# Rounding of 64-bit weights in three stages, with ScalarE's results in the score buffers, inside a fused attention and feed-forward kernel

## The chip, the cores and the metric

The kernel runs on one core of a Trainium2 chip. The metric is the device time of one execution in microseconds (us); the median of three runs is compared. A profile of one further execution shows what each engine did: PE (TensorE), DVE (VectorE), ACT (ScalarE), POOL (GpSimd) and the queue SP that issues the DMAs.

## The reference

The reference is a routed attention followed by a feed-forward block, all in fp32. There are 4 batches, 8 heads, 768 positions and a head dimension of 64.

```python
q_assign = argmax(q_n @ c_n)                    # 16 centroids per head; k_assign likewise
mask     = q_assign[:, :, :, None] == k_assign[:, :, None, :]
attn     = softmax(where(mask, q @ k.T / 8, -1e9))
x        = (attn @ v) laid out as (3072 tokens, 512)
h        = x @ w_in                             # 512 x 2048
out      = (h * sigmoid(1.702 * h)) @ w_out     # 2048 x 512
```

The two weight matrices reach the kernel as 64-bit floats. The kernel has to turn each into 32-bit floats before PE can use it, and it does that with integer operations on the two 32-bit halves.

## The kernel before

**Units and turns.** A *unit* is 128 keys against half of the queries (384) for a pair of heads. `scores(u)` is two matrix products into a PSUM tile `s` of 128x2x512 (two banks; the pool `ps_s` has two such tiles). For the first batch `part(u)` adds the mask with two small products of one-hot rows; `exps(u)` is ScalarE's exponential, which writes the SBUF tile `A`. For the later batches `exps` writes back into `s`, and `mask(u)` on VectorE makes `A` from it. GpSimd adds the six `A` of a group to `sum` (L430). `values(u)` multiplies `A` with the values; after the sixth unit ScalarE copies the result to `x` (L446). A *turn* `t` is two units; there are 96 turns, 24 for each batch, and three turns make a group.

**Order within a turn.** The program is an order written out by hand, turn by turn: every engine runs its instructions in the order in which this loop issues them. In a turn come the two `scores`, the two `part`, the two `exps`, then `mask`, the `values` of the turn before, and a list of preparations for later pairs of heads (`prep_turn`: transposes of queries and keys, L262 and L267; `prep_near` and `prep_assign`: the nearest centroid, L276 to L308; `prep_hot`: one-hot rows, L349 to L356). Once in three turns, at t = 4, 7, 10 and so on, `normalise(g)` sums over the keys with a product by ones (L453), takes VectorE's reciprocal `rec` (L456) and scales `x` (L458). `check(g)` then lets ScalarE form two sums over `rec` (L468, L470) that tell at the end whether the fast path holds. Last come the feed-forward chunks.

**Feed-forward.** Each half batch makes 28 chunks: 16 times `first` (four products with `w_in`, L487, then tanh, L492, and a product on VectorE, L494), and 12 times `second` (four products with `w_out`, L504). The chunks of a half batch enter the queue `ffn` at its last `normalise`, the first at t = 13; `rate` chunks (2.43) are taken per turn. Products, transposes and the rest share three PSUM banks `m` (`ps_m`).

**Rounding.** The weights are 32 pieces of 128x512, the first 16 of `w_in`. `load_w(i)` brings in a piece with its two halves interleaved (`raw`). `split_w` takes out the exponent `e` and the mantissa bits on VectorE (L159, L161) and converts both on ScalarE (L163, L165). `join_w` puts sign, exponent, and both parts of the mantissa together on VectorE (L171, L174, L177). All of it lies in SBUF. One `round_next()` is `split_w(i)` and then `join_w(i - 1)`. It is called once in most turns from t = 1 to 10, and from t = 12 two or three times a turn:

```python
        second = t >= TB // 2          # TB = 24
        if second:
            round_next()               # after the exps of the turn
...
        if second or t and t % 4 != 3:
            round_next()               # after preparations and normalise
...
        if second and t % 2:
            round_next()               # after the feed-forward chunks
```

`first` and `second` call `round_to(n)`, which rounds at once what a chunk needs and is not yet rounded.

Of the kernel before, what the change touches and what calls it, by code (L numbers as in the profile page):

```python
# [8 lines left out]
FP32 = mybir.dt.float32  # L9
BF16 = mybir.dt.bfloat16  # L10
I32 = mybir.dt.int32
U32 = mybir.dt.uint32
U8 = mybir.dt.uint8
AF = mybir.ActivationFunctionType
ALU = mybir.AluOpType
# [23 lines left out]
def fast(  # L39
# [21 lines left out]
    nc = tc.nc  # L61
# [4 lines left out]
    P = 128  # L66
    NJ = S // P
    HALF = S // 2
    NH = NJ // 2
# [3 lines left out]
    NF = DF // P  # L73
# [10 lines left out]
    wp = ctx.enter_context(tc.tile_pool(name="wp", bufs=3))  # L84
# [7 lines left out]
        name="dram", bufs=2, space=bass.MemoryType.DRAM))  # L92
    ps_s = ctx.enter_context(tc.tile_pool(name="ps_s", bufs=2, space=PS))
# [4 lines left out]
    def bank():  # L98
        return ps_m.tile([P, 512], FP32, name="m")

    def short():
        return tmp.tile([P, HALF], FP32, name="short")
# [14 lines left out]
    def load_v(p):  # L117
# [15 lines left out]
    WN = 512  # L133
    w_chunks = [
        (w[:, c, n:n + WN],
         src.bitcast(I32)[c * P:(c + 1) * P, 2 * n:2 * (n + WN)])
        for w, src, n_c, n_n in ((w_in, moe_w_in, NCH, DF),
                                 (w_out, moe_w_out, NF, DM))
        for n in range(0, n_n, WN) for c in range(n_c)]
    NW = len(w_chunks)  # L140
    w_raw, w_pow = {}, {}

    def load_w(i):
        if i < NW:
            t = wp.tile([P, WN, 2], I32, name="raw")
            nc.sync.dma_start(out=t.rearrange("p n t -> p (n t)"),
                              in_=w_chunks[i][1])
            w_raw[i] = t
# [2 lines left out]

    EXP = 0x7FF00000

    def split_w(i):

        hi = w_raw[i][:, :, 1]
        w = w_chunks[i][0]
        e = wp.tile([P, WN], I32, name="e")
        nc.vector.tensor_scalar(out=e, in0=hi, scalar1=EXP, scalar2=None,  # L159
                                op0=ALU.bitwise_and)  # L160
        nc.vector.tensor_scalar(out=w.bitcast(I32), in0=hi, scalar1=0xFFFFF,  # L161
                                scalar2=None, op0=ALU.bitwise_and)
        nc.scalar.activation(out=e, in_=e, func=AF.Relu, scale=8.0,  # L163
                             bias=low[:, 0:1])
        nc.scalar.activation(out=w, in_=w.bitcast(I32), func=AF.Copy,  # L165
                             scale=2.0 ** -20, bias=1.0)
        w_pow[i] = e

    def join_w(i):
        raw, e, w = w_raw.pop(i), w_pow.pop(i), w_chunks[i][0]  # L170
        nc.vector.scalar_tensor_tensor(  # L171
            out=e, in0=raw[:, :, 1], scalar=-2 ** 31, in1=e,
            op0=ALU.bitwise_and, op1=ALU.bitwise_or)
        nc.vector.scalar_tensor_tensor(  # L174
            out=w, in0=raw.bitcast(U32)[:, :, 0], scalar=2.0 ** -52, in1=w,
            op0=ALU.mult, op1=ALU.add)
        nc.vector.tensor_tensor(out=w, in0=w, in1=e.bitcast(FP32),  # L177
                                op=ALU.mult)

    w_done = [0]  # L180

    def round_next():
        i = w_done[0]
        if i < NW:
            load_w(i + 2)
            split_w(i)
        if 0 < i <= NW:
            join_w(i - 1)
        w_done[0] += 1

    def round_to(n):
        while w_done[0] <= min(n, NW):
            round_next()

    load_qk(1, 0)
    load_v(0)
# [8 lines left out]
    low = const.tile([P, 1], FP32, name="low")  # L205
# [25 lines left out]
                            op0=ALU.add)  # L231
# [3 lines left out]
    for a in range(2):  # L235
        nc.vector.tensor_scalar(out=cc[:, a, :], in0=cent,
                                scalar1=crec[:, 0:1], scalar2=None,
                                op0=ALU.mult)
# [5 lines left out]
    for a in range(2):  # L244
        rows = slice(a * D, (a + 1) * D)
        nc.vector.tensor_copy(
            out=cT[rows, :, a, :],
            in_=cps[rows, 0:P].rearrange("d (h a c) -> d h a c", a=2,
                                         c=NC)[:, :, a, :])
# [128 lines left out]
    def scores(u):  # L378
        g, kt = divmod(u, NJ)
        p, h = split(g)  # L380
        ps = ps_s.tile([P, 2, 512], FP32, name="s")
        for a in range(2):
            rows = slice(a * D, (a + 1) * D)
            nc.tensor.matmul(out=ps[:, a, 0:HALF],  # L384
                             lhsT=T[p, 1][rows, kt * P:(kt + 1) * P],
                             rhs=T[p, 0][rows, h * HALF:(h + 1) * HALF],
                             start=True, stop=(p >= HP))
        s_of[u] = ps[:, :, 0:HALF]

    def part(u):  # L390

        g, kt = divmod(u, NJ)
        p, h = split(g)
        if p >= HP:
            return
        for a in range(2):
            r = 32 * (2 * (p % 2) + a)
            nc.tensor.matmul(  # L398
                out=s_of[u][:, a, :],
                lhsT=hots[p // 2, 1][r:r + NC, kt * P:(kt + 1) * P],  # L400
                rhs=hots[p // 2, 0][r:r + NC, h * HALF:(h + 1) * HALF],
                start=False, stop=True)

    def exps(u):
        p, h = split(u // NJ)
        s = s_of[u]
        if p < HP:
            A_of[u] = ap.tile([P, 2, HALF], FP32, name="A")
        nc.scalar.activation(out=A_of[u] if p < HP else s, in_=s, func=AF.Exp,  # L409
                             scale=SCALE)  # L410
# [37 lines left out]
    def normalise(g):  # L448

        sm = sum_of.pop(g)  # L450
        ps = bank()
        for a in range(2):
            nc.tensor.matmul(out=ps[a * D:(a + 1) * D, 0:HALF], lhsT=ones,  # L453
                             rhs=sm[:, a, :], start=True, stop=True)
        rec = recs[g] = short()
        nc.vector.reciprocal(out=rec, in_=ps[:, 0:HALF])  # L456
        x = xT_of[g] = O_of.pop(g)
        nc.vector.tensor_tensor(out=x, in0=x, in1=rec, op=ALU.mult)  # L458
        if g % HP == HP - 1:
            ffn.extend(ffn_chunks(g // HP))  # L460

    recs = {}

    def check(g):


        rec = recs.pop(g)
        nc.scalar.activation(out=rec, in_=rec, func=AF.Copy,  # L468
                             accum_out=sums[:, 0, g:g + 1])
        nc.scalar.activation(out=rec, in_=rec, func=AF.Relu, bias=top[:, 0:1],  # L470
                             scale=-2.0 * LIMIT * LIMIT,
                             accum_out=sums[:, 1, g:g + 1])


    ffn = deque()
# [47 lines left out]
    TG = NJ // 2  # L523
    TB = 2 * HP * TG

    prep_at = {}
    for p in range(1, NPAIR):
        b, hp = divmod(p, HP)
        for i in range(2 if p == 1 else 0, len(PREP)):
            if p == 1:  # L530
                t = (i - 2) // 2
            elif b == 0:
                t = (hp - 2) * TG + 1 + i // 2
            else:
                t = b * TB + (-20, -8, -2, 1)[hp] + i
# [5 lines left out]
    def prep(p, i):  # L541
        if i == 0 and p:
            load_v(p)
        PREP[i](p)
        if i in (1, 3) and loads:
            load_qk(*loads.popleft())

    rate = (NF + NH * (NF // 4)) / (TB / 2 - 0.5)
    owed = 0.0
    for p, i in [(0, i) for i in range(6)] + [(1, i) for i in range(2)]:  # L550
        prep(p, i)
# [2 lines left out]
    for t in range(NT + 2):  # L554
        us = range(2 * t, 2 * t + 2) if t < NT else ()
        for u in us:
            scores(u)
        if t == 0:
            prep(0, 6)
        for u in us:  # L560
            part(u)
        for u in us:
            exps(u)
        second = t >= TB // 2
        if second:
            round_next()
        for u in us:
            mask(u)
        work = sorted(prep_at.get(t, ()), key=lambda w: PREP[w[1]] != prep_near)
        while work and PREP[work[0][1]] == prep_near:  # L570
            prep(*work.pop(0))
        if 1 <= t <= NT:
            for u in range(2 * t - 2, 2 * t):
                values(u)
        owed = owed + rate if ffn else 0.0
        g = (t - 2) // TG if t >= 2 and (t - 2) % TG == TG - 1 else None
        if g is not None and second:
            normalise(g)
        for p, i in work:
            prep(p, i)  # L580
        if g is not None and not second:
            normalise(g)
        if recs:
            check(*recs)
        if second or t and t % 4 != 3:
            round_next()
        while owed >= 1 and ffn:
            ffn.popleft()()
            owed -= 1
        if second and t % 2:  # L590
            round_next()


    ok = const.tile([P, 2, 2 * NPAIR], FP32, name="ok")
    nc.vector.tensor_scalar(out=ok, in0=sums, scalar1=LIMIT, scalar2=None,
                            op0=ALU.is_le)
    ok1 = const.tile([P, 1], FP32, name="ok1")
    nc.vector.tensor_reduce(out=ok1, in_=ok, axis=AX.XY, op=ALU.min)
    for _ in range(NF // 2):
# [7 lines left out]
                            op0=ALU.mult, op1=ALU.add)  # L607
# [445 lines left out]
```

## Time and profile before

| | |
|---|---|
| median of the runs | 1089.02 us (1088.73 to 1090.47) |
| the profiled execution's own time | 1089.2 us |
| its span, first to last instruction | 1087.3 us |
| PE busy | 1049.0 us (96%) |
| DVE busy | 490.8 us (45%) |
| ACT busy | 354.8 us (33%) |
| POOL busy | 296.9 us (27%) |
| granted TensorE clock, mean | 0.99 |

The time of the profiled execution is its span and 1.9 us around it. A busy share is taken over the whole span, while rounding ends at about 193 us; so the first 220 us, the 24 turns of the first batch, are read apart from the rest. A matrix product's row shows how long it was under way, which overlaps with the next; how fast PE can go is read from the distance between starts.

### The profile page before, as it was taken

Reading aid. Unit: us, or ns where it says so; the run is one execution under the profiler, and the core shown is the slowest. Engines: PE = TensorE matmul, PEld = TensorE weight load, DVE = VectorE, ACT = ScalarE, POOL = GpSimd, SP = SyncE. Lnnn points to the kernel's source line nnn. Section 1 sums busy time; section 2 is a strip of 40 time slices with the busy share of each in tenths; the row PEclk is TensorE's granted clock in tenths of the full one; section 3 lists DMA queues with packets and bytes.
Section 4 is the critical chain, followed back from the end, with each engine's and each line's share of the span. In section 5 each row is a group of like instructions: output and inputs, shape, how many; then the busy total and the mean of one; then the engine's idle time right before and its main releaser. Section 6 shows DMA issues by size and latency. Waiting matters only on the chain. (4 is left out here: it accounts for less than half of the span.)

```text
span 1087.3 us, 10456 instructions
## 1 busy us (share of the span) xinstructions
PE 1049.0 (96%) x3982; PEld 492.6 (45%) x3982; DVE 490.8 (45%) x744; ACT 354.8 (33%) x665; POOL 296.9 (27%) x168
## 2 busy tenths in 40 slices
PE   7878799999999999999999999999999999999997
PEld 3423344445544455444454445444554445444543
DVE  3889999225442344424453164423552344431200
ACT  3755555223422333223432233223332133311100
POOL 2644223213232333123231142222332333230000
PEclk9998899999999999999999999999999999999999
DMA  7623443110100010002100000010000000000000
GB/s 199 165 81 116 131 133 111 46 49 17 49 23 27 10 30 15 31 25 54 51 23 17 15 20 15 15 48 32 8 7 12 10 10 1 1 10 20 1 11 22
DMA packets 64813, 45.13 MB, mean 42 GB/s; under 512 B 51953, under 2 KB 57585, under 8 KB 64753
## 3 DMA queue, kind: packets, MB, share of 16 engines
q1 hardware_dynamic: 64608, 44.33, 14.3%
q8 instruction: 33, 0.54, 0.2%
q14 instruction: 28, 0.22, 0.1%
q10 hardware_dynamic: 144, 0.03, 0.0%
HBM read 38.04 MB, written 6.31 MB: 41 GB/s over the span
## 5 line engine op out<-in xcount | busy, mean ns | idle before, releaser
L430 POOL TENSOR_TENSOR sum<-sum,A 128x768 f32<-128x768 f32 x128 | 235.5, 1840 | 461.3 <-DVE A L420 364.1
L487 PE MATMUL m<-x,w_in 128*128 128x384 f32 x1024 | 347.1, 494 | 9.7 <-ACT T L267 4.4
L504 PE MATMUL m<-w_out,g 128*128 128x512 f32 x768 | 337.8, 594 | 0.7 <-ACT short L282 0.7
L420 DVE SCALAR_TENSOR_TENSOR A<-qb,code,s 128x384 f32<-128x384 uint8 x288 | 157.6, 609 | 274.6 <-ACT s L409 251.9
L487 PEld LDWEIGHTS m<-x,w_in 128*128 128x128 f32 x1024 | 192.2, 192 | 149.1 <-issue 16.3
L504 PEld LDWEIGHTS m<-w_out,g 128*128 128x128 f32 x768 | 143.3, 190 | 175.6 <-issue 171.5
L494 DVE SCALAR_TENSOR_TENSOR g<-g,m 128x384 f32<-128x384 f32 x128 | 70.0, 553 | 220.4 <-ACT g L492 220.3
L384 PE MATMUL s<-T,T 64*128 64x384 f32 x768 | 152.9, 517 | 9.7 <-ACT A L409 9.6
L409 ACT ACTIVATE s<-s 128x768 f32<-128x768 f32 x144 | 107.9, 792 | 136.0 <-PE s L384 136.0
L441 PE MATMUL o<-A,inv 128*64 128x384 f32 x768 | 146.3, 502 | 0.0
L492 ACT ACTIVATE g<-m 128x384 f32<-128x384 f32 x128 | 61.7, 487 | 196.4 <-PE m L487 196.3
L430 POOL TENSOR_TENSOR sum<-A 128x768 f32<-128x768 f32 x32 | 60.0, 1876 | 215.6 <-DVE A L420 179.5
L384 PEld LDWEIGHTS s<-T,T 64*128 64x128 f32 x768 | 66.6, 189 | 94.6 <-issue 52.2
L456 DVE RECIPROCAL short<-m 128x384 f32<-128x384 f32 x32 | 81.6, 2551 | 25.8 <-PE m L453 25.8
L441 PEld LDWEIGHTS o<-A,inv 128*64 128x64 f32 x768 | 46.8, 137 | 84.8 <-issue 84.1
L510 ACT ACTIVATE y<-m 128x512 f32<-128x512 f32 x24 | 14.3, 595 | 155.8 <-PE m L504 142.7
L468 ACT ACTIVATE short<-short 128x384 f32<-128x384 f32 x32 | 16.7, 523 | 111.2 <-DVE x L458 111.2
L409 ACT ACTIVATE A<-s 128x768 f32<-128x768 f32 x48 | 36.1, 804 | 22.0 <-PE s L398 22.0
L267 ACT COPY T<-m 128x384 f32<-128x384 f32 x64 | 29.7, 480 | 37.2 <-PE m L262 37.1
L262 PE MATMUL m<-ident,in 128*128 128x128 f32 x192 | 33.9, 298 | 3.1 <-ACT T L267 1.7
L163 ACT ACTIVATE e<-e,low 128x512 int32<-128x512 int32 x32 | 23.1, 722 | 28.8 <-DVE e L159 28.8
L262 PEld LDWEIGHTS m<-ident,in 128*128 128x128 f32 x192 | 21.5, 146 | 22.4 <-issue 11.9
(68 smaller groups left out, 373.5 us busy)
## 6 DMA issues: line engine op xcount, KB each, us to landing
raw<-in_moe_w_in_dram SPq DMA_DIRECT2D x16, 512.0 KB
raw<-in_moe_w_out_dram SPq DMA_DIRECT2D x16, 512.0 KB
in<-in_q_dram SPq DMA_DIRECT2D x32, 192.0 KB
in<-in_k_dram SPq DMA_DIRECT2D x32, 192.0 KB
inv<-in_v_dram SPq DMA_DIRECT2D x16, 384.0 KB
out_dram<-y SPq DMA_DIRECT2D x24, 256.0 KB
qb<-line SPq DMA_DIRECT2D x12, 192.0 KB
line<-row SPq DMA_DIRECT2D x12, 1.5 KB
```

The source lines that it names most:

```text
L262: nc.tensor.transpose(out=ps[:, n * P:(n + 1) * P], in_=qk_in[p, w][:, h * NH + n].rearrange("p a d -> p (a d)"), identity=ident)
L267: nc.scalar.copy(dst, ps[:, 0:HALF])
L384: nc.tensor.matmul(out=ps[:, a, 0:HALF], lhsT=T[p, 1][rows, kt * P:(kt + 1) * P], rhs=T[p, 0][rows, h * HALF:(h + 1) * HALF], start=True, ...
L409: nc.scalar.activation(out=A_of[u] if p < HP else s, in_=s, func=AF.Exp, scale=SCALE)
L420: nc.vector.scalar_tensor_tensor(out=A_of[u][:, a, :], in0=qcode[p][:, a, h * HALF:(h + 1) * HALF], scalar=code[p][:, kt % NH, 1, kt // NH ...
L430: nc.gpsimd.tensor_tensor(out=sum_of[g], in0=A_of[u - 1] if kt == 1 else sum_of[g], in1=A, op=ALU.add)
L441: nc.tensor.matmul(out=o_of[g][a * D:(a + 1) * D, 0:HALF], lhsT=v_in[p][:, a, kt, :], rhs=A[:, a, :], start=(kt == 0), stop=(kt == NJ - 1))
L456: nc.vector.reciprocal(out=rec, in_=ps[:, 0:HALF])
L487: nc.tensor.matmul(out=ps[:, 0:HALF], lhsT=w_in[:, c, f * P:(f + 1) * P], rhs=xT[c], start=(c == 0), stop=(c == NCH - 1))
L492: nc.scalar.activation(out=g, in_=ps[:, 0:HALF], func=AF.Tanh, scale=0.851)
L494: nc.vector.scalar_tensor_tensor(out=g, in0=g, scalar=1.0, in1=ps[:, 0:HALF], op0=ALU.add, op1=ALU.mult)
L504: nc.tensor.matmul(out=ps[:, 0:DM], lhsT=hs[f][:, n * P:(n + 1) * P], rhs=w_out[:, f, :], start=(f == 0), stop=(f == NF - 1))
```

## The change

`split_w` and `join_w` become three steps. `take_w` loads ahead and takes `e` and the mantissa bits out on VectorE. `part_w` is ScalarE's two conversions; their results go to a tile `r` that is taken from the score pool `ps_s` (name `s`), after the turn's exponentials, instead of being written in place in SBUF. `join_w` reads `r` from PSUM, writes an intermediate back to it, and ends in the weights. From t = 12 two pieces are rounded per turn (before: two or three), and before that one piece is joined in a turn that has one. Each step of a piece stands apart in the turn. `check` moves from the end of the turn that normalises to behind the exponentials of the next turn. For t below 24 two chunks are taken per turn (`SLOW`), from then on 2.43 (`RATE`).

```diff
-    def split_w(i):
-
+    w_at = [0, 0, 0]
+
+    def take_w():
+        i = w_at[0]
+        if i >= NW or i > w_at[2] + 1:
+            return
+        load_w(i + 2)
         hi = w_raw[i][:, :, 1]
-        w = w_chunks[i][0]
-        e = wp.tile([P, WN], I32, name="e")
+        e = w_e[i] = wp.tile([P, WN], I32, name="e")
         nc.vector.tensor_scalar(out=e, in0=hi, scalar1=EXP, scalar2=None,
                                 op0=ALU.bitwise_and)
-        nc.vector.tensor_scalar(out=w.bitcast(I32), in0=hi, scalar1=0xFFFFF,
-                                scalar2=None, op0=ALU.bitwise_and)
-        nc.scalar.activation(out=e, in_=e, func=AF.Relu, scale=8.0,
-                             bias=low[:, 0:1])
-        nc.scalar.activation(out=w, in_=w.bitcast(I32), func=AF.Copy,
-                             scale=2.0 ** -20, bias=1.0)
-        w_pow[i] = e
+        nc.vector.tensor_scalar(out=w_chunks[i][0].bitcast(I32), in0=hi,
+                                scalar1=0xFFFFF, scalar2=None,
+                                op0=ALU.bitwise_and)
+        w_at[0] += 1
+
+    def part_w():
+        i = w_at[1]
+        if i >= w_at[0]:
+            return
+        r = w_r[i] = ps_s.tile([P, 2, WN], FP32, name="s")
+        nc.scalar.activation(out=r.bitcast(I32)[:, 0, :], in_=w_e[i],
+                             func=AF.Relu, scale=8.0, bias=low[:, 0:1])
+        nc.scalar.activation(out=r[:, 1, :], in_=w_chunks[i][0].bitcast(I32),
+                             func=AF.Copy, scale=2.0 ** -20, bias=1.0)
+        w_at[1] += 1
 
-    def join_w(i):
-        raw, e, w = w_raw.pop(i), w_pow.pop(i), w_chunks[i][0]
+    def join_w():
+        i = w_at[2]
+        if i >= w_at[1]:
+            return
+        raw, e, r, w = w_raw.pop(i), w_e.pop(i), w_r.pop(i), w_chunks[i][0]
         nc.vector.scalar_tensor_tensor(
-            out=e, in0=raw[:, :, 1], scalar=-2 ** 31, in1=e,
+            out=e, in0=raw[:, :, 1], scalar=-2 ** 31,
+            in1=r.bitcast(I32)[:, 0, :],
             op0=ALU.bitwise_and, op1=ALU.bitwise_or)
         nc.vector.scalar_tensor_tensor(
-            out=w, in0=raw.bitcast(U32)[:, :, 0], scalar=2.0 ** -52, in1=w,
-            op0=ALU.mult, op1=ALU.add)
-        nc.vector.tensor_tensor(out=w, in0=w, in1=e.bitcast(FP32),
+            out=r[:, 1, :], in0=raw.bitcast(U32)[:, :, 0], scalar=2.0 ** -52,
+            in1=r[:, 1, :], op0=ALU.mult, op1=ALU.add)
+        nc.vector.tensor_tensor(out=w, in0=r[:, 1, :], in1=e.bitcast(FP32),
                                 op=ALU.mult)
+        w_at[2] += 1
...
+    RATE = (NF + NH * (NF // 4)) / (TB / 2 - 0.5)
+    SLOW = 2.0
...
-        second = t >= TB // 2
-        if second:
-            round_next()
+        part_w()
+        if recs:
+            check(*recs)
         for u in us:
             mask(u)
...
-        owed = owed + rate if ffn else 0.0
+        second = t >= TB // 2
+        owed = owed + (RATE if t >= TB else SLOW) if ffn else 0.0
...
         if g is not None and second:
             normalise(g)
+        if second:
+            join_w()
+            take_w()
         for p, i in work:
             prep(p, i)
         if g is not None and not second:
             normalise(g)
-        if recs:
-            check(*recs)
-        if second or t and t % 4 != 3:
-            round_next()
+        if second:
+            part_w()
+        join_w()
+        if not second and t and t % 4 != 3:
+            take_w()
         while owed >= 1 and ffn:
             ffn.popleft()()
             owed -= 1
-        if second and t % 2:
-            round_next()
+        if second:
+            take_w()
...
+    check(*recs)
```

## The prediction, made before the run

> **What bounds the kernel now.** I read the page's slices first, then the table of stretches cut at turn starts, then the waits of the first batch, its timeline, and the groups by form.
>
> ```profile
> PE   7878799999999999999999999999999999999997
> ...
> DVE  3889999225442344424453164423552344431200
> ...
> PEclk9998899999999999999999999999999999999999
> ```
>
> PE is full but for the first seven slices and the end. DVE is full in slices 3 to 6.
>
> ```profile
> core 0: us, PE busy (x) PEld busy (x) DVE busy (x) ACT busy (x) POOL busy (x), PEclk, DMA share, GB/s
> 41.10:82.10 41.00, 30.95 (x200) 12.52 (x198) 35.27 (x50) 24.74 (x49) 19.77 (x11) 0.99 0.45 120
> 92.40:138.40 46.00, 35.20 (x125) 16.49 (x123) 44.22 (x59) 21.74 (x42) 13.52 (x7) 0.89 0.43 128
> 138.40:219.30 80.90, 79.89 (x313) 36.70 (x312) 55.50 (x82) 35.74 (x66) 22.62 (x12) 1.00 0.32 93
> 219.30:968.90 749.60, 746.89 (x2787) 351.65 (x2786) 311.95 (x478) 230.06 (x434) 213.44 (x118) 1.00 0.08 23
> ```
>
> From 219.3 us (turn 24) PE is busy for 746.9 of 749.6 us: whatever this change does to ACT, DVE or POOL there is worth under 3 us. The case is decided in turns 3 to 23. At turns 14 to 16 (92.4 to 138.4) DVE is busy for 44 of 46 us, PE for 35.
>
> ```profile
> ACT short L468 <- DVE x L458: 20.2, 5, 6.0
> ...
> PE s L384 <- ACT A L409: 9.6, 5, 4.0
> ```
>
> These waits of 40 to 140 us show ACT standing in `check` for the reciprocal, and PE's scores then waiting for late exponentials.
>
> ```profile
> 82.02 0.69 DVE L171 SCALAR_TENSOR_TENSOR e<-raw,e 128x512 int32<-128x512 int32 x1
> 82.19 4.39 POOL L430 TENSOR_TENSOR sum<-sum,A 128x768 f32<-128x768 f32 x2 [3.78 <-ACT A L409]
> 82.62 2.29 DVE L174 SCALAR_TENSOR_TENSOR w_in<-raw,w_in 128x512 f32<-128x512 uint32 x1
> 84.95 2.18 DVE L177 TENSOR_TENSOR w_in<-w_in,e 128x512 f32<-128x512 f32 x1
> ```
>
> The same DVE step takes 0.69 us or 2.3: the long ones end with a POOL sum.
>
> ```profile
> L171 DVE SCALAR_TENSOR_TENSOR e<-raw,e 128x512 int32<-128x512 int32 x32 | 25.2, 787 | 0.0
> L163 ACT ACTIVATE e<-e,low 128x512 int32<-128x512 int32 x32 | 23.1, 722 | 28.8 <-DVE e L159 28.8
> L456 DVE RECIPROCAL short<-m 128x384 f32<-128x384 f32 x32 | 81.6, 2551 | 25.8 <-PE m L453 25.8
> L494 DVE SCALAR_TENSOR_TENSOR g<-g,m 128x384 f32<-128x384 f32 x128 | 70.0, 553 | 220.4 <-ACT g L492 220.3
> ```
>
> **What the change takes away.** (1) A join's three steps have one SBUF input each. L494 has that form (one input in PSUM) and its longest of 128 rows is 0.556 us, with POOL running: it is never held. Joins lose their stretching: between 82 and 195 us L171, L174 and L177 hold 62.5 us in 75 steps, against 0.69 each: 11 us of DVE gone. (2) `check` no longer makes ACT wait (20.2 us of ACT in 40 to 140). (3) 2 instead of 2.5 pieces a turn.
>
> **What it costs in durations.** ACT's conversions go to PSUM: L409 takes 0.792 us into PSUM, 0.804 into SBUF, so nothing. A join step from PSUM: L494 is 0.553 us for 384 elements, and 128 more at 1.04 ns make 0.686, the same as L171 unstretched (0.68). No row of DVE writes PSUM; I take it as free, and 0.06 us each way (2 us over 32) as the bounds. [...]
>
> **What is moved at no cost.** `load_w` now issues its DMA behind the join that frees the buffer, so SP stands there less (four loads held it 16.1 us from 80.74); DVE waited 0.6 us for `raw` in all, and the loads of q, k and v behind it come no later. `check` keeps one of three `short` tiles for a turn more, and the last `check` lands behind the last turn's chunks: ACT is busy for 230 of 750 us there and PE is covered by the feed-forward; uncovered, 1.3 us for each. The four chunks put off lengthen the tail by 13.7 us and the turns before it shrink by as much, since PE does both without a gap.
>
> **What it costs in waits, which decides.** `ps_s` has two tiles, and `r` takes the one of the turn's first unit. The built order shows it: PE's second `scores` of the next turn waits for the last step of the join, and from t = 12, with two pieces a turn, both do. Behind that product queue all of PE's part, values, normalise and chunks, and ACT's exponentials behind them. Before, a score tile was free as soon as ACT had read it. So a loop closes through three engines. From the start S of a turn's second scores, by distances between starts: scores 0.75, to the first exponential 0.42, two exponentials 1.38, conversions 0.63 and 0.62, join 0.60 + 0.72 + 0.69, two hand-overs of 0.05: 5.9 us to the next S. PE's work in a bare turn is 3.3 (scores 1.49, part 0.43, values 1.42). What DVE does ahead of the join in its queue lengthens the loop:
>
> - `prep_assign` with `prep_near` (t = 3, 6): ACT's copy L282 stands behind the conversions, S + 3.7; transposes and hand-overs 1.15, DVE's five steps 2.65, join 2.05: 9.5 us. At t = 9, without `near`: 8.0.
> - normalise (t = 7, 10): values end at S + 2.6, ones 0.9, reciprocal and scaling 3.1, join 2.05: 8.7, with one-hot work ahead 10.0 at t = 7, and 8.9 at t = 10.
> - t = 4 has no piece (6.3), but its reciprocal delays the next `take_w`: 8.4 at t = 5. t = 8: no piece, 4.1. t = 11: 5.9. t = 12: 6.4, with L446 ahead.
> - t = 13: normalise and two pieces, 8.7 and take 0.65, conversion 1.3, join 2.05: 12.7.
>
> From S = 30.7 at t = 3 (before: 29.75) these eleven add up to 89.7 us: S = 120.4 at t = 14, against 92.4 + 0.75 = 93.2 before. **27.2 us are lost here.**
>
> From t = 14 an ordinary turn is 5.9 + 0.65 + 1.3 + 2.05 = 9.9 us (PE's work: 3.3 and two chunks of eight L487 at 0.323, 8.5); one with normalise 12.7 (t = 16, 19, 22). At t = 21 L446 waits for a chunk's product that frees its `x` tile, with ACT's second conversion behind it: 11.2. At t = 23 the last chunk needs piece 31, joined out of turn: 15.5. Five ordinary, three of 12.7, and the two: 114.3 us to t = 24. Before: 93.2 to 220.0 is 126.8 us, but with four more `second` chunks, eight L504 at 0.429 each, 13.7 us, which the changed kernel does later on a full PE: 113.1. **Lost: 1.2 us**, so the relief of DVE is spent on the loop.
>
> Together 28.4 us. PE's clock comes on top. By the records of the granted clock, PE's idle times of 4.0 us (to 82.1), 2.9 (to 114.5) and 4.1 (to 130.1) each brought a stretch at half clock, of 6.8, 3.4 and 6.8 us; one of 2.4 us (to 100.4) did not. The changed kernel has about ten idle times of 2.5 to 5 us up to t = 14 where PE's pieces lie on the loop: 1.2 us each, 3.5 where values and ones are in it. Between 0 and 18 us; I take 8, as not all of a turn's pieces will fall into the slow stretch. [...]
>
> 1089.2 + 28.4 + 8 = 1125.6 us by the profiled execution; it stands 0.2 above the median, and with some of the smallest waits hidden I say 1124.
>
> **Rivals.** *The relief wins (faster).* If the scores' wait is met early, because ACT and DVE run ahead of PE as before, the stall of turns 14 to 16 goes: 46.0 us for 29.3 of PE work (seven chunks at 2.58, three bare turns at 3.34, 1.2 for ones and transposes), 16.7 us, so 1072. For it: DVE is full there and `check` is off ACT's way. Against it: it needs a join to end before PE has done the first scores of the next turn, 3.4 us after S, and the loop takes 5.9 at the least; it decides from a loop under PE's own 3.3 to 5.3. *Half of the stalls are covered*: 14 us lost, no drop of the clock, 1103. [...] *Cancelled*: within 2 us, 1089. That the waits are not there at all is excluded by the built order.
>
> **Chances.** Forecast 0.66 (1110 to 1142: 1117.6 and between 0 and 18 us of clock, and some 7 us either way for the writes to PSUM and for turns whose waits I count twice or miss), half covered 0.14, worse 0.10, relief 0.08, cancelled 0.02. The range 1100 to 1142 leaves out the last three. About 0.2% (2.2 us) is what a measurement can tell from no change: faster 0.08, same 0.02, slower 0.90.
>
> **What would show it.** In the waits: PE `s` L394 on DVE `w_in` L195 with 25 us or more, none on ACT's `A`. Turn starts: t = 14 near 119 us and t = 24 near 235 to 242. L188, L192, L195 at 0.69 us without stretched rows. More half clock between 35 and 120 us. [...]

## The result, and the profile after

The changed kernel takes 1145.34 us (median of four runs, 1141.75 to 1146.3), the kernel before 1088.93 (four runs, 1088.73 to 1090.47) on the same chip: a ratio of 1.0509, 95% interval 1.0484 to 1.0533. The direction was forecast, the size was not: 56 us were lost where 35 were forecast, and 1145 lies above the range of 1100 to 1142. The profiled execution took 1146.3 us, span 1144.4, mean granted clock 0.965 (before 0.990).

The first two lines that answer to those of before are from the page's slices:

```profile
PE   7667598889999999999999999999999999999997
...
PEclk9867798998999999999999999999999999999999
```

Counted from one, PE's holes in slices 2 to 5 are deeper than before and slices 7 to 9 have new ones, and in slices 2 to 10 the granted clock falls to 0.6 to 0.9. From slice 11 on both lines read as before. The stretches from turn 4, from turn 14 and from turn 24 (a turn begins with its first scores):

```profile
core 0: us, PE busy (x) PEld busy (x) DVE busy (x) ACT busy (x) POOL busy (x), PEclk, DMA share, GB/s
35.30:134.90 99.60, 64.74 (x290) 23.54 (x289) 47.88 (x69) 35.61 (x64) 31.11 (x17) 0.76 0.23 65
134.90:260.70 125.80, 107.75 (x404) 47.62 (x404) 78.91 (x137) 58.50 (x107) 30.84 (x17) 0.91 0.34 101
260.70:1010.00 749.30, 747.27 (x2771) 352.01 (x2771) 306.61 (x472) 226.11 (x428) 208.41 (x116) 1.00 0.08 23
```

Turns 4 to 13 take 99.6 us; before they took 57.6 (34.8 to 92.4). No engine is full there: PE is busy for 65 us of them, DVE for 48. That fits a chain that goes around through several engines. The clock over those turns is 0.76 on the average. Turn 14 starts at 134.9 us (forecast: near 119), turn 24 at 260.7 (235 to 242). From turn 24 on PE is busy for 747.3 of 749.3 us, as before.

The table of waits between 25 and 265 us says who closes the chain:

```profile
PE s L394 <- DVE w_in L195: 39.4, 12, 5.4
...
PE s L394 <- DVE w_out L195: 9.9, 6, 2.7
...
PE m L514 <- DVE w_out L195: 4.6, 2, 2.7
```

PE's scores stand 49.3 us for the last step of a join, and no wait of the scores for ACT's `A` is left. And the joins themselves, by form:

```profile
L192 DVE SCALAR_TENSOR_TENSOR s<-raw,s 128x512 f32<-128x512 uint32 x32 | 22.3, 696 | 2.2
...
L188 DVE SCALAR_TENSOR_TENSOR e<-raw,s 128x512 int32<-128x512 int32 x32 | 21.9, 685 | 42.5 <-ACT s L179 42.5
...
L195 DVE TENSOR_TENSOR w_in<-s,e 128x512 f32<-128x512 f32 x16 | 11.1, 691 | 0.5
```

All 96 steps take 0.69 us, none is stretched; DVE waits 42.5 us ahead of them for ACT's conversions, so DVE is no longer what is full.

### The profile page after: what moved, and what is told of

Same layout as the page of the kernel before. It is cut to its first block, busy times and chain, and to the rows that moved or that the text cites. A ratio compares the mean times of both kernels' runs of the same rounds, so it can differ in the third digit from the quotient of the medians.

```text
span 1144.4 us, 10589 instructions
## 1 busy us (share of the span) xinstructions
PE 1074.9 (94%) x3982; PEld 498.0 (44%) x3982; DVE 466.3 (41%) x744; ACT 355.8 (31%) x665; POOL 291.5 (25%) x168
## 5 line engine op out<-in xcount | busy, mean ns | idle before, releaser
L440 POOL TENSOR_TENSOR sum<-sum,A 128x768 f32<-128x768 f32 x128 | 232.4, 1815 | 491.3 <-DVE A L430 367.1
L497 PE MATMUL m<-x,w_in 128*128 128x384 f32 x1024 | 342.4, 490 | 0.3 <-ACT T L277 0.3
L497 PEld LDWEIGHTS m<-x,w_in 128*128 128x128 f32 x1024 | 191.5, 191 | 137.0 <-issue 10.3
L394 PE MATMUL s<-T,T 64*128 64x384 f32 x768 | 163.3, 537 | 49.4 <-DVE w_in L195 39.4
L451 PE MATMUL o<-A,inv 128*64 128x384 f32 x768 | 158.8, 538 | 0.0
L394 PEld LDWEIGHTS s<-T,T 64*128 64x128 f32 x768 | 67.5, 194 | 140.3 <-issue 69.7
L440 POOL TENSOR_TENSOR sum<-A 128x768 f32<-128x768 f32 x32 | 57.8, 1806 | 248.2 <-DVE A L430 185.9
L451 PEld LDWEIGHTS o<-A,inv 128*64 128x64 f32 x768 | 49.7, 145 | 93.1 <-issue 93.1
L520 ACT ACTIVATE y<-m 128x512 f32<-128x512 f32 x24 | 14.3, 597 | 172.6 <-PE m L514 156.5
L188 DVE SCALAR_TENSOR_TENSOR e<-raw,s 128x512 int32<-128x512 int32 x32 | 21.9, 685 | 42.5 <-ACT s L179 42.5
L177 ACT ACTIVATE s<-e,low 128x512 int32<-128x512 int32 x32 | 22.2, 694 | 33.1 <-DVE e L163 33.1
```

The source lines that it names most:

```text
L394: nc.tensor.matmul(out=ps[:, a, 0:HALF], lhsT=T[p, 1][rows, kt * P:(kt + 1) * P], rhs=T[p, 0][rows, h * HALF:(h + 1) * HALF], start=True, ...
L440: nc.gpsimd.tensor_tensor(out=sum_of[g], in0=A_of[u - 1] if kt == 1 else sum_of[g], in1=A, op=ALU.add)
L451: nc.tensor.matmul(out=o_of[g][a * D:(a + 1) * D, 0:HALF], lhsT=v_in[p][:, a, kt, :], rhs=A[:, a, :], start=(kt == 0), stop=(kt == NJ - 1))
L497: nc.tensor.matmul(out=ps[:, 0:HALF], lhsT=w_in[:, c, f * P:(f + 1) * P], rhs=xT[c], start=(c == 0), stop=(c == NCH - 1))
```

## The experiments

Each run's time stands beside runs of the kernel before on the same chip (1087.9 to 1089.0 us).

**1. PE's clock kept up by fillers.** Transposes that nobody reads fill PE's wait ahead of the second scores.

```diff
-        for u in us:
+        for j, u in enumerate(us):
+            warm(FILL.get((t, j), 0))       # n transposes into a bank()
             scores(u)
```

> The changed kernel, with 6 to 34 transposes of the identity (0.133 us each at full clock, into a spare bank of the m pool, read by nobody) ahead of PE's second scores in the turns where PE stood waiting for the join (t = 4, 6, 7, 8, 10, 11, 13, 14, 17, 20, 22; 1.3 to 4.5 us in a turn, some 0.6 us under the wait seen). Nothing else moves. Theory 1 (the loop through the score tile has the length I worked out, and what came on top is PE's own pieces of the loop at half clock): the granted clock stays at 1.0 between 35 and 230 us, the turn starts return to my list plus 3.2 us for one stretched take_w at t = 4: S at t = 14 is 123 us (changed kernel: 138.7), t = 24 near 237 (262.1), time 1117 to 1125. Theory 2 (the half clock only goes with the waits, and the loop is longer for another reason on DVE or ACT): time 1138 to 1146 and the same turn starts. If the fillers themselves run into the chain: over 1146.

1132.49 us, ratio 1.0391 (1.0373 to 1.0408). Between the two theories: 13 us came back, but five stretches of half clock were left, one of them where the filler at t = 6 itself stood 4.2 us for its bank, behind ACT's copy. So the filler was made free of the banks, with products that add zero to the score tile just filled:

```diff
+            for _ in range(n):
+                nc.tensor.matmul(out=pad[u - 1], lhsT=cT[0:D, 0, 1, :],
+                                 rhs=ident[0:D, :], start=False, stop=False)
```

> The changed kernel, with 5 to 35 small products ahead of PE's second scores (t = 4, 6, 7, 8, 10 to 14, 16, 17, 19, 20, 22) that add zero times the identity (64 rows, 16 columns of weights, 128 moving columns, about 0.11 us each) to the score tile that the turn has just filled, so that they wait for no bank; 42 transposes ahead of t = 14's first scores as in the first such run. That run left three stretches at half clock before t = 15 (a filler at t = 6 stood 4.2 us for its own bank). Theory 1 (what came on top of my list is half clock on the loop): no half clock, or one stretch, between 35 and 225 us, turn 14 starts near 120 us (134.9 in the changed kernel, 128.6 in the first run with fillers), time 1118 to 1127. Theory 2 (the clock is worth no more than the first run showed): 1130 or more at a clock of 1.0 up to t = 22. If products this small don't keep the clock up, the half clock stays and the time is 1140 or more.

1146.07 us, ratio 1.0530 (1.0513 to 1.0548), at a clock of 0.994. A miss of mine: a product is two instructions, 0.224 us, twice what I had reckoned. At t = 8 the join ended at 85.11 us and the fillers at 88.38. The fillers had taken the join's place in the chain, so the run tells nothing of the clock. With about half as many:

> The run with zero products again, with fewer: the last one had them run 2.5 us past the join's end in most turns (a product took 0.224 us, twice what I had reckoned), which filled PE but lengthened the loop itself. Now 3, 15, 16, 13, 17, 13, 17, 8 and 9 of them at t = 3, 4, 6, 7, 8, 10, 11, 12 and 13, 10 at t = 14 behind 34 transposes, and 2 to 9 at t = 16 to 20 and 22, so that they end 0.5 to 1 us ahead of the join. Theory 1 (on top of the listed loop came half clock on PE's pieces): clock 1.0 from 35 to 225 us, turn 14 starts at 120 to 124 us (134.9), turn 24 near 241 (260.7), time 1122 to 1128. Theory 2 (the half clock costs little, the loop is longer for another reason): turn 14 after 128 us, time 1132 or more with the clock at 1.0.

1125.72 us, ratio 1.0361 (1.0337 to 1.0384). The same three stretches (turns 4 to 13, 14 to 23, the rest):

```profile
36.30:120.10 83.80, 74.70 (x540) 41.34 (x539) 47.88 (x69) 35.44 (x64) 31.20 (x17) 1.00 0.26 77
120.10:241.00 120.90, 109.49 (x484) 51.98 (x484) 78.70 (x137) 58.14 (x107) 30.90 (x17) 0.98 0.34 105
241.00:990.00 749.00, 746.97 (x2773) 352.15 (x2773) 306.50 (x472) 226.12 (x428) 209.27 (x116) 1.00 0.08 23
```

DVE, ACT and POOL do the same work (47.9, 35.4 and 31.2 us in turns 4 to 13) in 83.8 instead of 99.6 us, with the clock at 1.00; only a stretch in turn 23 is left. Turn 14 starts at 120.1 us and turn 24 at 241.0. Theory 1 holds: **half clock costs the changed kernel 1145.3 - 1125.7 = 19.6 us** between the medians. The two were run on different chips: set against the kernel before on its own chip it is 56.4 - 37.8 = 18.6 us by the medians, and 16 by the ratios 1.0509 and 1.0361. So the price is 16 to 20 us. How it gets into the chain is seen in turn 6. Its second scores start at 59.04 us in the changed kernel:

```profile
59.04 1.65 PE L394 MATMUL s<-T,T 64*128 64x384 f32 x4 [4.83 <-DVE w_in L195]
...
61.22 1.51 ACT L419 ACTIVATE A<-s 128x768 f32<-128x768 f32 x2 [2.08 <-PE s L408]
...
62.81 2.83 PE L451 MATMUL o<-A,inv 128*64 128x384 f32 x8
...
65.57 0.90 PE L297 MATMUL m<-ident,short 128*128 128x128 f32 x3
...
70.59 0.69 DVE L195 TENSOR_TENSOR w_in<-s,e 128x512 f32<-128x512 f32 x1
```

and at 57.06 in the kernel with fillers (its lines stand one further down, L395 for L394):

```profile
57.06 0.92 PE L395 MATMUL s<-T,T 64*128 64x384 f32 x4 [1.23 <-DVE w_in L195]
...
58.35 1.51 ACT L420 ACTIVATE A<-s 128x768 f32<-128x768 f32 x2 [1.18 <-PE s L409]
...
59.12 1.51 PE L452 MATMUL o<-A,inv 128*64 128x384 f32 x8
...
61.54 0.55 PE L297 MATMUL m<-ident,short 128*128 128x128 f32 x3 [0.91 <-ACT short L292]
...
66.20 0.69 DVE L195 TENSOR_TENSOR w_in<-s,e 128x512 f32<-128x512 f32 x1
```

From the scores to the exponentials it is 2.2 us at half clock and 1.3 at full clock, to the transposes L297 6.5 against 4.5, to the join's last step 11.6 against 9.1. ACT's and DVE's own pieces are alike.

**2. No score tile.** The conversions go back in place in SBUF; stages, places and cadence stay.

```diff
-        r = w_r[i] = ps_s.tile([P, 2, WN], FP32, name="s")
-        nc.scalar.activation(out=r.bitcast(I32)[:, 0, :], in_=w_e[i],
+        nc.scalar.activation(out=e, in_=e,
...
```

> The changed kernel, with ScalarE's two conversions written in place in SBUF as before (no score tile is taken; the three stages, their places, the late check and 2 chunks a turn stay). Theory 1 (the score tile is the whole loss): PE's wait for the join is gone, PE loses no more than before in turns 3 to 13, clock near 0.99, time 1075 to 1092, the lower end if the late check and the fewer pieces relieve turns 14 to 16. Rival (the order in three stages and the fewer chunks cost by themselves): 1105 or more, with waits of PE on g, x or the weights in turns 14 to 23.

1111.89 us, ratio 1.0200 (1.0183 to 1.0218). PE's scores wait for no join any more, and 33 us of the 56 are gone. But 23 us stay: the rival's figure. So the score tile is the larger part of the loss, not all of it. The joins read two SBUF inputs again in this run, and some of their steps take up to 2.30 us instead of 0.69 (the second step at 38.64 us, with a POOL sum under way from 38.17 on), so the 33 us are what is left after that.

**3. The check alone**, moved behind the next turn's exponentials in the kernel before:

> The kernel before, with only the check of the row sums moved behind the exponentials of the next turn. Theory 1: ACT no longer stands 20.2 us for the reciprocal between 40 and 140 us, part of PE's 9.6 us of waits for late exponentials goes: 1080 to 1088. Rival (ACT's stand was time it had): 1088 to 1090. A loss is expected by neither.

1087.33 us, ratio 0.9991 (0.9981 to 1.0001): not to be told from no change. ACT's stand for the reciprocal was time that it had.

**4. The cadence too**: the run before, with two pieces a turn and two chunks a turn below t = 24.

> The kernel before with the late check, two pieces a turn from t = 12 (no third call in odd turns) and two chunks a turn before t = 24: all of the change but the three stages and the score tile. Theory 1 (what is left of the loss with the conversions in place, 23 us, is the cadence: the last pieces of w_out come late and chunks force them): PE waits for w_out in turns 22 to 24 with 8 us or more, time 1097 to 1112. Theory 2 (it is the three stages: conversions and takes in ACT's and DVE's queue in other places, and joins stretched there): 1078 to 1090, PE full from turn 17 on.

1090.43 us, ratio 1.0014 (1.0004 to 1.0023). Check and cadence together cost 1.5 us. Theory 1 falls: what stays without the score tile, 1111.9 - 1090.4 = 21.5 us, comes from the three stages.

**5. Which stage.** Of the three stages only ScalarE's, in place, with VectorE's order as before (`part_w` behind the next turn's exponentials):

> The kernel before with the late check, two pieces and two chunks a turn (1090.4 us), and of the three stages only ScalarE's: a piece's two conversions, in place in SBUF, are issued behind the next turn's exponentials or ahead of the next call, instead of right behind the take. VectorE's order stays that of before (take, then the join of the piece before). Theory 1 (with the conversions in place, 21 us of loss remain because ScalarE in its fixed order stands for the late take, 64 us in that run, with exponentials and copies for PE behind it): 1100 to 1112. Theory 2 (it is VectorE's order: the take behind a join that GpSimd's sums stretch, each join one place earlier): 1086 to 1094.

1095.51 us (five runs, 1092.0 to 1097.6), ratio 1.0063 (1.0043 to 1.0083): 5.1 us more than in 4, between the theories and nearer the second. Then run 2 with the take ahead of the join:

```diff
+            take_w()
             join_w()
-            take_w()
...
-        join_w()
         if not second and t and t % 4 != 3:
             take_w()
+        join_w()
```

> The changed kernel with the conversions in place, and the take ahead of the join in every turn instead of behind it. Theory 1 (ScalarE stands for a take that lies behind join and reciprocal on VectorE): ScalarE's wait for the take falls from 64 us to under 40, time 1096 to 1106. Theory 2 (the joins themselves, stretched, delay what PE waits for): little changes, 1107 to 1114.

1105.12 us (four runs, 1098.8 to 1108.3), ratio 1.0127 (1.0085 to 1.0168): 6.8 us come back by the medians, with several us of spread. In run 2, ACT's wait for the take between 25 and 265 us is

```profile
ACT e L177 <- DVE e L163: 64.1, 26, 5.6
```

against 28.8 in 17 before; it falls to 45.7 with the take first, not under the 40 that I had expected. That this wait is what costs is not shown. Run 4, which loses 1.5 us, has nearly as much of it:

```profile
ACT e L163 <- DVE e L159: 56.2, 22, 6.6
```

and PE's scores wait for late exponentials no longer in run 2 (6.7 us) than in run 4 (7.2). What PE does wait longer for in run 2 is DVE's results:

```profile
PE m L496 <- DVE g L503: 4.9, 3, 3.4
...
PE m L462 <- DVE qb L363: 4.4, 1, 4.4
PE m L332 <- DVE g L503: 4.1, 1, 4.1
...
PE m L271 <- DVE qb L363: 3.8, 1, 3.8
```

That makes 8.2 us for the one-hot copy `qb` (1.3 in run 4) and, with two short waits more, 9.4 for `g` (2.6). From turn 3 to turn 25 run 2 takes 211.8 us and run 4 188.7: PE idles 14.4 us longer, and is busy 8.7 us longer with as many products, since 37.5 us are at half clock instead of 17.1.

The join's own place was tried twice. Without a join in turns 3, 7 and 11:

```diff
-        join_w()
+        if second or t and t % 4 != 3:
+            join_w()
```

> The run with the conversions in place, without a join in the turns in which no piece is taken (t = 3, 7, 11), as before the change. Theory 1 (23 us remained there because the join, 5.1 us when GpSimd's sums hold it, now falls into turns 3, 7 and 11, ahead of the one-hot copy that PE's transposes wait for): PE's wait of 3.8 us at t = 4 goes and that of 4.4 at t = 7 shrinks, time 1100 to 1106. Rival (what remains is ScalarE's conversions behind the exponentials and DVE's takes, in every turn): 1108 to 1113.

1109.50 us, ratio 1.0199 (1.0181 to 1.0218). The wait at t = 4 went as expected (the turn fell from 11.3 to 6.3 us), but turn 6 grew from 10.1 to 12.5, for ACT's copy of T (L276). And with the join right behind the conversions:

```diff
         for u in us:
             mask(u)
+        join_w()
+        if t >= TB // 2:
+            take_w()
...
-        if second:
-            join_w()
-            take_w()
```

> The changed kernel with conversions in place in SBUF (as in the second run) and the first join of a turn right behind them on DVE, ahead of nearest-centroid steps and the reciprocal. No score tile, so no loop. Theory 1 (in the in-place run the stretched join stood ahead of the one-hot copy and the reciprocal, and PE's transposes and chunks waited for those): the same stretched steps now stand ahead of the nearest-centroid steps, so little is gained: 1105 to 1114. Rival (the place of the join in DVE's queue is what cost there): 1090 to 1100.

1116.69 us, ratio 1.0244 (1.0212 to 1.0275): no gain, even a little above the range of theory 1; the rival falls.

**6. The loop shortened, score tile kept.** The same edit in the changed kernel:

> The changed kernel, with the first join of a turn issued on DVE right behind the conversions (ahead of the nearest-centroid steps and of the reciprocal; for t from 12 with the take_w behind it). The score tile is still taken. Theory 1 (loop from S over scores, part, exponentials, conversions, join; what DVE has ahead of the join lengthens it): every turn from t = 3 to 12 falls to 5.9 to 6.5 us or to PE's own work where that is more, S at t = 14 near 104 us (138.7), half clock much rarer as PE then idles under 2 us a turn, time 1103 to 1115. Rival (the second conversion or the take, not DVE's queue ahead of the join, sets the loop): under 10 us are gained, 1136 or more.

1122.87 us, ratio 1.0305 (1.0288 to 1.0322): 22 us back, between the two. Turns 3, 4 and 11 fell to 4.6 to 7.0 us (from 6.9, 13.5 and 9.8), but t = 6 fell only from 13.7 to 12.7 and t = 12 rose from 5.2 to 11.7. The timeline of turn 12 has the reason:

```profile
88.90 2.54 DVE L466 RECIPROCAL short<-m 128x384 f32<-128x384 f32 x1
...
93.42 2.02 DVE L163 TENSOR_SCALAR e<-raw 128x512 int32<-128x512 int32 x1
...
99.16 1.65 PE L394 MATMUL s<-T,T 64*128 64x384 f32 x4 [6.35 <-DVE w_in L195]
```

The take stands behind the reciprocal and the scaling, and conversions, join and PE's scores stand behind the take. The scaling (L468, at 91.48 us) and the take's first step last 2.02 us each here, while POOL sums run from 91.28 to 95.16 us, against 0.56 and 0.42 unstretched. With the take early too:

```diff
         join_w()
-        if t >= TB // 2:
+        if t >= TB // 2 or t and t % 4 != 3:
             take_w()
...
-        join_w()
-        if not second and t and t % 4 != 3:
-            take_w()
+        if second:
+            join_w()
```

> The changed kernel with the first join and the take both right behind the conversions in every turn (the run with the join alone moved left PE waits of 4.8 us at t = 6 and 6.4 at t = 12, where the take stood behind the reciprocal). The score tile is still taken. Theory 1 (the loop is scores, part, exponentials, conversions, join, and whatever stands ahead of them on DVE and ACT): turns 3 to 12 at 5.9 to 6.5 us or PE's own work, turn 14 starts near 105 us (114.1 with the join alone moved), time 1106 to 1115. Rival (the first-stage take was not it): 1119 to 1125.

1118.62 us, ratio 1.0283 (1.0266 to 1.0300). Turn 6 falls to 7.7 and turn 14 starts at 107.6 us (expected 105), yet only 4 us come back in the whole (8.1 between the two profiled executions): the second join of turn 13 still has normalise ahead of it on DVE, and PE's second scores of turn 14 wait 4.9 us for it.

**7. A version that might beat both**: run 4 with the third piece in odd turns again.

> The kernel before with the late check and two chunks a turn before t = 24, but with before's third call in odd turns, so that the last pieces come in time. Theory 1: the wait of 4.0 us for w_out at t = 22 that two pieces a turn brought goes, and fewer chunks relieve turns 14 to 16: 1081 to 1088, a little under before. Rival (the third piece fills DVE in turns 14 to 16 as before, and chunks were not its limit): 1087 to 1091.

1094.05 us, ratio 1.0051 (1.0037 to 1.0065): a miss for both. It does away with the wait for `w_out` at t = 22, but PE now also stands ahead of L487 at t = 15, 19 and 21 (2.8, 1.8 and 2.7 us). No version tried is faster than the kernel before by more than the measurement can tell.

## Why the prediction was wrong in size

**The loop: right in kind, 7.8 us short.** The list of distances from S to S, made from rows of before alone, can be held against the trace with the clock kept up, turn for turn from t = 3:

| t | 3 | 4 | 5 | 6 | 7 | 8 | 9 | 10 | 11 | 12 | 13 | sum |
|---|---|---|---|---|---|---|---|---|---|---|---|---|
| forecast, us | 9.5 | 6.3 | 8.4 | 9.5 | 10.0 | 4.1 | 8.0 | 8.9 | 5.9 | 6.4 | 12.7 | 89.7 |
| clock kept up | 9.9 | 6.4 | 9.5 | 9.9 | 10.1 | 4.2 | 7.7 | 9.1 | 6.3 | 6.8 | 12.7 | 92.6 |
| changed kernel | 9.9 | 9.3 | 9.5 | 12.3 | 13.0 | 7.4 | 7.7 | 11.6 | 6.6 | 6.8 | 14.3 | 108.4 |

From t = 14 to 24 it was 114.3 forecast, 118.6 with the clock kept up, and 123.4 in the changed kernel. With the start 0.6 us later, the list was short by 0.6 + 2.9 + 4.3 = 7.8 us: 28.4 + 7.8 + 1089.2 = 1125.4, and 1125.7 was measured. Of the 7.8, 1.1 is t = 5, whose take was stretched (below), 2.2 are the five ordinary turns after t = 14 (10.3 us each, forecast 9.9), and 2.1 is t = 23; that one still has half clock. This is a little more than the 7 us that the range allowed.

**The clock: the step that failed.** The sum took 8 us, between 0 and 18; 16 to 20 were measured, 19.6 between the medians. "Not all of a turn's pieces will fall into the slow stretch" is what went wrong. Before, three stretches held 17 us at half clock; now, between 25 and 265 us, eleven hold 75. Of PE's 13 stalls there of 2 us or more, all but one had half clock begin before their end or within 1 us after it, and the stretch fell on PE's own pieces of the loop: by the table, turns 4, 6, 7, 8, 10 and 13 are longer by 1.6 to 3.1 us each. Turns 3 to 13 lose 108.4 - 92.6 = 15.8 us in this way, nearly all that the upper bound held, and turns 14 to 23 another 123.4 - 118.6 = 4.8, which the prediction's count of idle times "up to t = 14" left at nothing. The fillers took away ten of the eleven stretches: 19.6 / 10 = 2.0 us for each on the average, inside the 1.2 to 3.5 that the prediction had for one. So the count (about ten forecast up to t = 14; eight stretches came by then and three later) and the price of one were near; the discount to 8 us was what failed. Neither error leaves the range alone: 1125.6 + 7.8 = 1133.4 and 1117.6 + 19.6 = 1137.2; both together do.

**The rivals.** "Worse" (chance 0.10, 1150 us) stood for a clock that falls at every stall and a POOL sum that catches a take in most turns. It came nearest, for the clock: it fell at 12 of the 13 stalls above. The takes did not go that way: one piece's was caught, in turn 4, with POOL sums (L440) under way from 51.69 to 55.76 us,

```profile
52.06 2.04 DVE L163 TENSOR_SCALAR e<-raw 128x512 int32<-128x512 int32 x1
54.02 2.02 DVE L165 TENSOR_SCALAR w_in<-raw 128x512 int32<-128x512 int32 x1
```

and every other step of a take took 0.43 us at the most. "The relief wins" (1072) is refuted beyond its condition: even with no wait of the scores for a join, the three stages take 1111.9 us. The prediction laid the whole loss on the score tile. What delays the loop there (a take behind the reciprocal, a join behind the centroid steps) costs time without it as well; through which engine is open. In the sum these delays were part of the loop's turns, so the list held and the explanation behind it was too narrow. One reading of the prediction is off and nothing rests on it: counted from one, PE is below 0.9 in the first five slices, not seven, and DVE's full slices are the fourth to the seventh.

**Durations: right.** A join step from PSUM takes 0.685 us (forecast 0.686), the same as the unstretched step from SBUF before (0.684, the median of L171). One that also writes PSUM takes 0.696, within the 0.06 us that the prediction allowed without a row for it, and ACT's conversions into PSUM 0.69 and 0.60. **Moved at no cost: right.** The check, the two pieces and the four chunks put off cost 1.5 us together by run 4, and turns from 25 on lose the same as before.

**Open.** Of the 21.5 us that the three stages cost without a score tile, ACT's place accounts for 5.1 by itself, and 6.8 return with the take ahead of the join. These two shares come from runs that spread over 6 and 10 us, so their size is rough. The rest is not assigned: joins still stretched there by POOL's sums (up to 2.3 us a step in the trace of run 2) and their place earlier in the turn are argued, not shown; the two runs on the join's place only moved the waits. Part of the 21.5 us is the clock again, by the 8.7 us more of busy PE in run 2; no run with the clock kept up separates it there.

## What to carry to other kernels

A buffer of an early engine that is lent to a late one turns a straight pipeline into a loop; its length can be added up from the rows of the old trace before anything is built, everything that stands ahead of it in each engine's fixed order included, and here that sum came out 7.8 us short over 21 turns, under half a microsecond a turn. If PE then idles inside that loop, count the fall of its clock at the upper bound: here the slow stretch fell on the loop's own pieces in most of the turns with a stall, at 2.0 us for a stretch on the average. A test that fills PE's idle time separates the two, if the fillers end before the wait does.

## What the runs showed of the hardware

In the traces of the two kernels the granted clock is 1.0 or 0.5, and all starts of half clock (5 before, 13 after) lie whole multiples of 3.413 us apart, to within 0.001 us; the stretches last 3.41, 6.83, 10.24 or 13.65 us, but for the last of each trace, which the end of the run cuts short. In all twelve traces without fillers the starts lie on such a grid. What goes with a fall in these traces is how busy PE is in a slice of that grid, not the length of one unbroken pause. In the two kernels, between 27 and 270 us, PE's records cover at most 0.41 of 14 of the slices at full clock, and all 14 were followed by half clock; they cover at least 0.46 of the 101 others, and none of these was. Over the twelve traces, of the slices with less than 0.42, 74 of 74 were followed by half clock; of the 660 others, 4 were, all between 0.43 and 0.46. (The bound of 0.42 was drawn from these same traces.) So in the changed kernel a pause of 2.69 us that fell mostly into one slice (t = 17, busy 0.41) brought a stretch of 6.8 us, and one of the same length that straddled two (t = 20, busy 0.61 and 0.60) brought none.
